# The order in which TensorE reads the keys in the row-maximum passes of an attention kernel

## The chip, the cores and the metric

The kernel runs on one core of a Trainium2 chip. The metric is the device time of one execution in microseconds (us), the median over the executions shown. The engines of the core are called PE (TensorE, matrix products), ACT (ScalarE), DVE (VectorE), POOL (GpSimd) and SP (SyncE, which here issues DMAs). PE takes a stationary operand through a weight load (PEld) and streams a moving operand against it, column by column, from the on-chip memory SBUF into a bank of PSUM; a bank holds 512 float32 columns on each of 128 partitions.

## The reference, cut to what matters

```python
def _B_ref(x, wqkv, wo):          # x: 1 x 2048 x 1024, H = 32 heads of Dh = 32
    qkv = (x @ wqkv).reshape(B, S, 3, H, Dh).transpose(2, 0, 3, 1, 4)
    q, k, v = qkv[0], qkv[1], qkv[2]
    scores = jnp.einsum("bhqd,bhkd->bhqk", q, k) * (Dh ** -0.5)
    p = softmax(scores, axis=-1)
    o = jnp.einsum("bhqk,bhkd->bhqd", p, v)
    return o.transpose(0, 2, 1, 3).reshape(B, S, D) @ wo

g = sigmoid((x * gate_w).sum(-1, keepdims=True))
return g * _A_ref(x, A_wqkv, A_wo) + (1 - g) * _B_ref(x, B_wqkv, B_wo)
```

`_A_ref` is a linear attention of the same size (feature map, keys times values, a division by the sum of keys). Everything is float32. The softmax of block B subtracts the largest score of each row, so the kernel needs the maximum over 2048 keys for each query and head. A maximum doesn't depend on the order in which the keys come.

## The kernel before

The program is written by a planner in Python: several streams of work (generators) each offer their next step, the planner keeps a modelled time for every engine (`T`), and it appends the step that is furthest behind its due time and whose operands are modelled to be there. What comes out is one fixed order of instructions for each engine. The modelled price of one 512-column product is `MM = 0.2275`. Nothing of this runs on the chip; there the engines follow their queues and wait on semaphores.

The first stage (lines below 850) makes queries, keys and values of block B. The main stage runs four streams side by side:

- `maxima()`, the passes of the row maxima. For each of the 32 heads it goes through 64 pairs of a block of 128 queries (`t`, 16 of them) and a block of 512 keys (`j`, 4 of them). A pass is one product on line 1263: the stationary operand is a 128 x 128 block of the stacked queries `q`, the moving operand is `k[:, j * C:(j + 1) * C]`, 512 neighbouring keys (C = 512), and the result fills one PSUM bank. On line 1268 DVE reduces the bank to one maximum per query. Queries and keys are stored as high and low parts, stacked on the 128 partitions, in the type float32r.
- `heads_()` with `attend()`: the products of keys with queries on line 1405, the exponential on ACT (line 1408), sums of the exponentials on POOL (line 1490) and DVE (line 1506), and the products with the values on line 1555. The latter are plain float32; each of the program's 2048 products runs as two passes, which makes 4096 instructions, and four of them with 32 columns of weights each share the array.
- `linear()`: the projections of block A and the rest of block B's values, on lines 153, 156 and 158, three products for each of eight row blocks, with transposes on line 1049 and the small key-value products on line 938.
- `output()`: the last projection.

The maxima of a head are made about one head and 12 passes (`LEAD`) ahead of its exponentials. After the 64 passes of a head, `rows(h)` turns the 16 columns of maxima with one small transpose on line 1280, and two short DMAs write them into the stacked operand, so that the products on line 1405 come out with the maximum subtracted. A pass takes a bank with `take`, and `give` sets it free when the reduction on DVE has read it; seven banks go around (six of a ring and one that is lent while it is idle). The lines around the change:

## Time and profile before

| | |
|---|---|
| time, median of 2 runs | 2806.33 us (2805.76 to 2806.9) |
| span of the profiled execution, first to last instruction | 2803.6 us |
| mean granted clock of TensorE | 1.000 |
| first and last start of a pass of the row maxima (line 1263) | 432.0 and 2572.4 us |
| passes of the row maxima | 2048, busy 739.0 + 62.8 us |
| reductions behind them (line 1268) | 2048, busy 1314.3 us, 684 ns each |

The page gives, for an engine, the time in which at least one of its instructions is under way, and its share of the span. In its list of groups a row names the source line, the engine, the operation, the tile written and the tiles read, the shapes and the count; after the first bar come the busy time of the whole group in us and the mean of one in ns, after the second the idle time of the engine just before these instructions and what ended it. Products overlap in the array, so the busy time of one is longer than the interval from one start to the next. No separate time of the profiled execution is given beside its span; what lies around the span is taken from the runs' median.

### The profile page before, as it was taken

The numbers are of one execution on the slowest core, as the hardware profiler recorded it, in microseconds if no ns is written. First come the engines' busy times: TensorE is split into PE (matmuls) and PEld (weight loads), VectorE is DVE, ScalarE is ACT, GpSimd is POOL, SyncE is SP. The second block draws the span as 40 slices with busy tenths as digits, with TensorE's granted clock in tenths as the row PEclk, the third lists the DMA queues.
The fourth block names the chain that finished last, engine by engine and source line by source line (L and its number), as shares of the span: only waits on it lengthen the run. The fifth ranks groups of instructions, "written<-read, shape, count | busy, mean of one in ns | idle before, by whom it ended". The sixth has DMA issues, their size and how long they took to land.

```text
span 2803.6 us, 46986 instructions
## 1 busy us (share of the span) xinstructions
PE 2794.3 (100%) x15880; PEld 2040.4 (73%) x15880; DVE 2327.5 (83%) x3745; ACT 1640.2 (59%) x3095; POOL 2104.4 (75%) x1150
## 2 busy tenths in 40 slices
PE   9999999999999999999999999999999999999999
PEld 8888888776677767777667777776676667666687
DVE  7978956888888888888888888888887888886688
ACT  5334323666676666666666676676666666666522
POOL 0642543799999999999899988889889988888000
PEclk9999999999999999999999999999999999999999
DMA  8997979433444334333433444455575555544774
GB/s 286 314 327 232 319 225 287 153 99 107 104 120 109 99 95 125 99 102 97 135 98 102 107 129 133 148 175 178 176 222 145 147 159 150 144 122 150 253 234 152
DMA packets 403340, 459.52 MB, mean 164 GB/s; under 512 B 106894, under 2 KB 234894, under 8 KB 401308
## 3 DMA queue, kind: packets, MB, share of 16 engines
q1 hardware_dynamic: 381084, 419.03, 48.6%
q0 software_dynamic: 22016, 37.50, 6.3%
q8 instruction: 126, 2.06, 0.3%
q14 instruction: 114, 0.93, 0.1%
HBM read 314.31 MB, written 127.66 MB: 158 GB/s over the span
## 4 chain that ended last, share of the span: by engine, by line
PE 91%; DMA 3%; DVE 1%; issue 1%; SPq 0%; ACT 0%; ACTq 0%; DVEq 0%
PE bank L1405 17%; PE bank L1263 17%; PE bank L1555 16%; PE bank L153 13%; PE bank L158 13%; PE bank L156 13%; PE bank L1327 1%; PE bank L1049 1%; DMA big<-wv 1%; SPq L170 0%; DMA big<-ra 0%; DMA xs<-big 0%; PE bank L938 0%; DMA mid<-in_xT 0%; DMA extra<-in_xT 0%
## 5 line engine op out<-in xcount | busy, mean ns | idle before, releaser
L1490 POOL TENSOR_TENSOR big<-big,big 128x512 f32<-128x512 f32 (+2 forms) x694 | 1642.0, 2370 | 106.9 <-ACT big L1408 63.8
L1268 DVE TENSOR_REDUCE mx<-bank 128x1 f32<-128x512 f32 x2048 | 1314.3, 684 | 301.1 <-PE bank L1263 297.5
L1408 ACT ACTIVATE big<-bank 128x512 f32<-128x512 f32 x2048 | 1180.0, 602 | 427.8 <-PE bank L1405 362.4
L1405 PE MATMUL bank<-big,big 128*128 128x512 f32 x1888 | 741.5, 394 | 0.1
L1263 PE MATMUL bank<-big,big 128*128 128x512 f32 x1888 | 739.0, 391 | 0.0
L153 PE MATMUL bank<-big,big 128*128 128x512 f32 x1576 | 616.0, 391 | 2.8 <-ACT big L302 1.2
L156 PE MATMUL bank<-big,big 128*128 128x512 f32 x1576 | 614.2, 390 | 0.0
L158 PE MATMUL bank<-big,big 128*128 128x512 f32 x1572 | 613.2, 390 | 0.2 <-DMA big<-xs 0.2
L1555 PE MATMUL bank<-big,mid 128*32 128x512 f32 x4096 | 454.2, 593 | 0.0
L1405 PEld LDWEIGHTS bank<-big,big 128*128 128x128 f32 x1888 | 354.0, 188 | 124.7 <-issue 47.4
L1263 PEld LDWEIGHTS bank<-big,big 128*128 128x128 f32 x1888 | 354.5, 188 | 73.7 <-ACT big L1408 1.4
L153 PEld LDWEIGHTS bank<-big,big 128*128 128x128 f32 x1576 | 296.0, 188 | 69.5 <-ACT big L302 2.6
L158 PEld LDWEIGHTS bank<-big,big 128*128 128x128 f32 x1572 | 295.1, 188 | 63.6 <-DVE big L297 1.0
L156 PEld LDWEIGHTS bank<-big,big 128*128 128x128 f32 x1576 | 295.9, 188 | 61.3 <-DVE big L297 0.2
L1555 PEld LDWEIGHTS bank<-big,mid 128*32 128x32 f32 x4096 | 143.6, 110 | 264.3 <-issue 264.0
L1506 DVE TENSOR_TENSOR bank<-bank,big 128x512 f32<-128x512 f32 x364 | 252.2, 693 | 5.5 <-ACT big L1408 3.3
L302 ACT CAST big<-mid 128x512 fp32r<-128x512 f32 (+1 forms) x157 | 92.9, 618 | 122.5 <-DVE mid L1674 66.0
L1486 POOL TENSOR_TENSOR big<-big,big 128x1536 f32<-128x1536 f32 (+1 forms) x31 | 123.4, 3980 | 40.3 <-ACT big L1408 40.1
L153 PE MATMUL bank<-big,xh 128*128 128x512 f32 x376 | 147.0, 391 | 0.6 <-DVE mx L1268 0.6
L158 PE MATMUL bank<-big,xh 128*128 128x512 f32 x376 | 146.9, 391 | 0.3 <-DMA xh<-xs 0.3
L156 PE MATMUL bank<-big,xh 128*128 128x512 f32 x376 | 146.8, 390 | 0.0
L1563 ACT COPY mid<-bank 128x512 f32<-128x512 f32 x32 | 18.8, 587 | 212.8 <-PE bank L1555 205.8
(165 smaller groups left out, 2226.4 us busy)
## 6 DMA issues: line engine op xcount, KB each, us to landing
big<-xs SPq DMA_DIRECT2D x288, 256.0 KB
big<-qk SPq DMA_DIRECT2D x690, 64.0 KB
xh<-xs SPq DMA_DIRECT2D x144, 256.0 KB
qk<-mid SPq DMA_DIRECT2D x128, 256.0 KB
big<-oA SPq DMA_DIRECT2D x84, 256.0 KB
xs<-big SPq DMA_DIRECT2D x64, 256.0 KB
oA<-mid SPq DMA_DIRECT2D x64, 256.0 KB
big<-big POOLq DMA_DIRECT2D x50, 256.0 KB, 5.4
```

Of the source, the lines that this page charges most:

```text
L153: yield nc.tensor.matmul(ps, sh, mh_, start=(kt == 0), stop=False)
L156: yield nc.tensor.matmul(ps, sh, ml_, start=False, stop=(late and last))
L158: yield nc.tensor.matmul(ps, sl, mh_, start=False, stop=last)
L302: nc.scalar.copy(hi, src)
L1263: nc.tensor.matmul(bank[b], q[:, t % TPC * P:(t % TPC + 1) * P], k[:, j * C:(j + 1) * C], start=True, stop=True)
L1268: nc.vector.tensor_reduce(m[:, t, j:j + 1], bank[b], AX.X, ALU.max)
L1405: nc.tensor.matmul(bank[b], k[:, t * P:(t + 1) * P], q_cols(h, j), start=True, stop=True)
L1408: nc.scalar.activation(pr_t[i][:, j * C:(j + 1) * C], bank[b], AF.Exp, scale=SCALE)
L1486: nc.gpsimd.tensor_add(lacc[:, :qp], pr(0)[:, :qp], pr(1)[:, :qp])
L1490: nc.gpsimd.tensor_add(lacc[:, sl], lacc[:, sl], pr(t)[:, sl])
L1506: nc.vector.tensor_add(lacc[:, qp:] if t == NT - 1 else l_b[:, :n], l_b[:, :n], src)
L1555: nc.tensor.matmul(av_b[j * DH:(j + 1) * DH, :], v[:, t, :], pr(t)[:, j * C:(j + 1) * C], start=(t == 0), stop=(t == NT - 1))
```

## The change

Each of the passes of line 1263 reads its 512 keys in an order that depends on the head's number modulo 8, which I call its kind:

| kind | order in which the 512 keys enter |
|---|---|
| 0 | as before, one after the other |
| 1, 2, 3, 4 | with a step of 2, 4, 16 or 32 keys: first keys 0, n, 2n and so on, then 1, n + 1 and so on |
| 5 | pairs of neighbours, each second pair first (keys 0, 1, 4, 5, ...), then the others |
| 6 | runs of 16 neighbours, each second run first, then the others |
| 7 | as before, but as two products of 256 keys into the two halves of the bank |

The result is written to the bank from column 0 to column 511 in every kind, so for kinds 1 to 6 the scores stand in the bank in another order. The reduction reads all 512 of them as before. There are 32 heads, so each kind has 4 heads of 64 passes. A key is 4 bytes. The planner's price of a pass is left at `MM`. This is the whole diff:

```diff
+    def key_order(kind, to, keys):
+
+        if kind == 7:
+            return [(to[:, :HC], keys[:, :HC]), (to[:, HC:], keys[:, HC:])]
+        if kind in (1, 2, 3, 4):
+            n = (2, 4, 16, 32)[kind - 1]
+            return [(to.rearrange("p (n c) -> p n c", n=n), keys.rearrange("p (c n) -> p n c", n=n))]
+        if kind in (5, 6):
+            e = (2, 16)[kind - 5]
+            return [(to.rearrange("p (n c e) -> p n c e", n=2, e=e), keys.rearrange("p (c n e) -> p n c e", n=2, e=e))]
+        return [(to, keys)]
+
     def maxima():
...
                 end = use("pe", MM, free[b])
-                nc.tensor.matmul(bank[b], q[:, t % TPC * P:(t % TPC + 1) * P], k[:, j * C:(j + 1) * C],
-                                 start=True, stop=True)
+                rows_ = q[:, t % TPC * P:(t % TPC + 1) * P]
+                keys = k[:, j * C:(j + 1) * C]
+                for to, mov in key_order(h % 8, bank[b], keys):
+                    nc.tensor.matmul(to, rows_, mov, start=True, stop=True)
                 s_done[0] += 1
                 fill(end + LATE)
```

Here HC is 256. In the changed file the passes are on line 1278 instead of 1263, the reduction is on 1282 instead of 1268, and line 1405 has become 1419.

On PE, where the passes of head 6 end and those of head 7 (kind 7) begin, the program before has these instructions; a name like bank_244 is a PSUM bank, the two names after the arrow are the stationary and the moving operand, and the last column is the size of the result:

```order
L1263 MATMUL bank_239<-big_207,big_206 128x512
L1405 MATMUL bank_241<-big_208,big_209 128x512
L1263 MATMUL bank_244<-big_209,big_208 128x512
L156 MATMUL bank_238<-big_222,big_210 128x512
L158 MATMUL bank_238<-big_222,big_210 128x512
L1405 MATMUL bank_243<-big_208,big_209 128x512
L1263 MATMUL bank_240<-big_209,big_208 128x512
```

The changed program has at the same place on PE:

```order
L1278 MATMUL bank_239<-big_207,big_206 128x512
L1419 MATMUL bank_241<-big_208,big_209 128x512
L1278 MATMUL bank_244<-big_209,big_208 128x256 x2
L156 MATMUL bank_238<-big_222,big_210 128x512
L158 MATMUL bank_238<-big_222,big_210 128x512
L1419 MATMUL bank_243<-big_208,big_209 128x512
L1278 MATMUL bank_240<-big_209,big_208 128x256 x2
```

Each pass of head 7 has become two instructions with the same operands, and nothing else has moved; the passes of head 6 (the first row) look as before, since the order of their keys isn't part of such a row.

On DVE, which reduces the banks that these passes fill, a piece of the program before reads as follows (mx is the tile of the maxima, big_4148 one of the exponentials):

```order
L1268 TENSOR_REDUCE mx_199<-bank_242 128x1
L1268 TENSOR_REDUCE mx_199<-bank_239 128x1
L1268 TENSOR_REDUCE mx_199<-bank_238 128x1
L1506 TENSOR_TENSOR bank_245<-bank_245,big_4148 128x512
L1268 TENSOR_REDUCE mx_199<-bank_243 128x1
```

The same piece in the changed program:

```order
L1282 TENSOR_REDUCE mx_199<-bank_242 128x1
L1282 TENSOR_REDUCE mx_199<-bank_239 128x1
L1282 TENSOR_REDUCE mx_199<-bank_238 128x1
L1520 TENSOR_TENSOR bank_245<-bank_245,big_4148 128x512
L1282 TENSOR_REDUCE mx_199<-bank_243 128x1
```

Only the line numbers differ: the same banks are reduced in the same order.

## The prediction

> **What bounds the kernel now.** I read the page from the top: the busy shares of the engines, the 40 slices, the chain that ended last, the costliest groups.

> ```profile
> span 2803.6 us, 46986 instructions
> PE 2794.3 (100%) x15880; PEld 2040.4 (73%) x15880; DVE 2327.5 (83%) x3745; ACT 1640.2 (59%) x3095; POOL 2104.4 (75%) x1150
> PE   9999999999999999999999999999999999999999
> PEclk9999999999999999999999999999999999999999
> PE 91%; DMA 3%; DVE 1%; issue 1%; SPq 0%; ACT 0%; ACTq 0%; DVEq 0%
> ```

> TensorE (PE) is busy in every slice, at the full granted clock, and carries 91% of the chain. Outside its busy time there are only 2803.6 - 2794.3 = 9.3 us of the whole span. So whatever lengthens a matmul has nowhere to hide, and whatever another engine gains or loses below PE's pace costs nothing. A "busy" PE could still be a PE that waits inside its pipeline, so I checked the pace in the timeline of PE alone, in a stretch of twenty full-size matmuls in a row (first and last row shown):

> ```profile
> 1007.55 0.39 PE L1405 MATMUL bank<-big,big 128*128 128x512 f32 x1
> ...
> 1011.86 0.39 PE L156 MATMUL bank<-big,big 128*128 128x512 f32 x1
> ```

> The starts lie (1011.86 - 1007.55) / 19 = 0.2268 us apart. Each is busy for 0.39 us, because the next enters while the last still drains; the price of one more matmul is thus its interval, not its busy time. The passes of the row maxima are line 1263, and the reduction that waits for each is line 1268. These groups, from the page and from the list of groups with shapes kept apart, carry the rest of the argument:

> ```profile
> L1268 DVE TENSOR_REDUCE mx<-bank 128x1 f32<-128x512 f32 x2048 | 1314.3, 684 | 301.1 <-PE bank L1263 297.5
> L1263 PE MATMUL bank<-big,big 128*128 128x512 f32 x1888 | 739.0, 391 | 0.0
> L1263 PE MATMUL bank<-big,extra 128*128 128x512 f32 x160 | 62.8, 393 | 0.0
> L1555 PE MATMUL bank<-big,mid 128*32 128x512 f32 x4096 | 454.2, 593 | 0.0
> L938 PE MATMUL bank<-mid,mid 128*32 128x32 f32 x1024 | 15.7, 199 | 0.0
> L1263 PEld LDWEIGHTS bank<-big,big 128*128 128x128 f32 x1888 | 354.5, 188 | 73.7 <-ACT big L1408 1.4
> ```

> Passes of line 1263 number 1888 + 160 = 2048: 32 heads by 64. Their moving operand is 512 neighbouring keys of 4 bytes. VectorE (DVE) waits 297.5 us in all for these matmuls; PE never waits for VectorE there (0.0). The next view gives the busy time by stretch; this row is a steady one:

> ```profile
> 600.00:1000.00 400.00, 399.97 (x2585) 280.92 (x2576) 347.06 (x587) 263.62 (x509) 371.85 (x184) 1.00 0.38 103
> ```

> After the length come PE, PE's weight loads, VectorE, ScalarE and GpSimd: PE is full, VectorE at 347.06 of 400, GpSimd at 371.85 of 400. GpSimd is the next engine behind PE, 7% short of it.

> **The change part by part.** The kind is the head's number modulo 8, so each kind has 4 heads and 4 x 64 = 256 passes. Kind 0 is unchanged. The planner still charges a pass MM = 0.2275, so the order of work on all engines stays as it was; only kind 7 puts a second matmul behind the first. Nothing moves past a queue, no DMA is added, and no wait is added: the reduction still waits for one release, that of the last matmul into its bank. The maximum doesn't depend on the order of the keys, and the bank is still written from column 0 to 511.

> *Kind 7, two matmuls of 256 keys.* It adds 256 matmuls and 256 weight loads. A 32-column product (line 938) takes 199 ns and a 512-column one 391, so a column costs (391 - 199) / 480 = 0.40 ns. Of the interval of 227 ns the columns are 205, and 22 are a fixed part that each half pays anew: 2 x (102 + 22) = 248, which is 21 ns more. 256 x 0.021 = 5.5 us. The lower bound is 0, if the fixed part overlaps. The upper bound is one weight load (188 ns, the last row above) in the open for each pair: 256 x 0.188 = 48 us, plus the 5.5. What decides between them is the shortest run of full-width loads in the trace, the four transposes of 128 columns, each with a load of its own:

> ```profile
> 1708.28 0.60 PE L1049 MATMUL bank<-ident,mid 128*128 128x128 f32 x4
> 1708.63 0.48 PE L1263 MATMUL bank<-big,big 128*128 128x512 f32 x1
> ```

> Four loads and matmuls are in before 0.35 us have passed, and the matmul behind them runs 0.48 instead of 0.39, so about 0.44 us for four. A load every 0.11 us keeps up with halves of 0.124 us. I take 5.5 us.

> *Kinds 1 to 6, one matmul with stepped keys.* Instructions, columns and weight loads stay as they are. What can change is the pace at which the moving operand comes out of SBUF. The trace of before has no matmul that reads with a step, so the price is bounded from both sides. Lower bound: 0, since the array still takes 512 columns, and nothing in fewer. A gain is excluded: nothing about a step makes 512 columns fewer. Upper bound from the nearest row: line 1555, the one whose columns enter at a slower pace. Four such passes of 512 columns share the array, and 4 x 454.2 / 4096 = 0.4436 us go by per group, against 0.2268 for line 1263: 0.217 us more. By its busy time it is 593 - 391 = 202 ns more. So a stream of 512 keys at half pace costs 0.20 to 0.22 us more; I call it 0.21.

> I take a mechanism in which a read of the memory brings several neighbouring keys at a time and a stream that uses only one of them drops to half pace. It is an assumption that this trace can't show. For it speaks that line 1263 must be given 512 x 4 bytes in 0.2268 us, 9.0 bytes a nanosecond in each partition, where one stream of line 1555 is given 512 x 4 in 0.4436, 4.6. No single stream of the trace is seen to get more than the first figure, and that one is of neighbouring keys. With steps of 4, 16 and 32 (kinds 2, 3, 4) no two keys in turn come from the same four, so I charge these the 0.21; with a step of 2, in pairs, and in runs of 16 (kinds 1, 5, 6) at least two in turn lie in one group of four, so I charge these nothing. The charge is 3 x 256 x 0.21 = 161.3 us, with 0 and 0.217 x 768 = 167 as ends for these three kinds. What would hide it would be slack of PE, and of that there are the 9.3 us above.

> [...]

> *Sum.* 2803.6 (the span of the execution shown) + 5.5 + 161.3 = 2970.4. The median of the runs shown, 2806.33, is 2.7 above that span, for what lies around it; I add it: **2973 us**, 5.9% more. In the slow heads GpSimd and VectorE get more slack, not less. The steps are in neighbouring heads, and this row of the source line that runs once a head gives their length:

> ```profile
> L1280 PE MATMUL bank<-ident,mneg x32: 270/271/275, 492.0 to 2574.4; 128*16 128x128 f32 x32
> ```

> (2574.4 - 492.0) / 31 = 67.2 us a head; a head of kinds 2 to 4 would take 64 x 0.21 = 13.4 us more, about 80.6.

> **The rivals.**

> *Steps are free* (ends on the other side: not slower). The operand's path reads ahead and gathers any 512 keys at the full pace. Then only kind 7 pays: 2803.6 + 5.5 + 2.7 = 2812. For it: PE never waits for an operand anywhere in this page, and the four streams of line 1555 together get 4 x 4.6 = 18.5 bytes a nanosecond from SBUF, so the memory has twice the supply of one stream. Against it: those are four streams with a path each, not one. The point from which it decides: the 2% mark is 56 us, less 5.5 for kind 7, over 768 passes, so a wide step that costs under 66 ns.

> *Only the widest steps pay*, 16 and 32: 2812 + 512 x 0.21 = 2919. It needs a reach of more than four keys; the page speaks neither for nor against it.

> *All stepped kinds pay half pace*, 1 to 5, because the pace of line 1263 is already the most that whole groups of neighbours give: 2812 + 1280 x 0.21 = 3081. The fixed 22 ns beside 205 ns of columns say that contiguous reads leave little to spare.

> *The same limit, in full*: if a group of four neighbours takes the time of four columns whatever of it is used, a step of 2 and pairs cost double and steps of 4 and more four times the columns: 2812 + 512 x 0.21 + 768 x 3 x 0.205 = 3392. Against it: no row shows a stream slower than half pace.

> *Kind 7 with its loads in the open* and free steps: 2812 + 48 = 2860, held off by the four transposes. That the change does nothing is no rival: a stepped read can't be folded into a plain one while the bank is written in order.

> **How the numbers follow.** Forecast 0.32; free 0.31; only the widest 0.11; all at half pace 0.09; four times 0.14; open loads 0.02; faster 0.01, for which nothing speaks. A measurement of this kernel can tell about 2% (56 us) from no change. Slower by more: 0.32 + 0.11 + 0.09 + 0.14 = 0.66; within: 0.31 + 0.02 = 0.33; faster: 0.01. The likeliest's own range is 2955 (0.19 a pass) to 3025 (0.217, and kind 7 at its upper bound). The range on record reaches to the free case and to all kinds at half pace, 2806 to 3085, and holds 0.32 + 0.31 + 0.11 + 0.09 + 0.02 = 0.85 of the cases; what is left out is the fourfold case and the faster one.

> **What would show it right or wrong.** In the changed profile the passes of the maxima should fall into groups: kinds 0, 1, 5, 6 with starts 0.227 us from the matmul before, kinds 2, 3, 4 about 0.44, halves of kind 7 about 0.124. Their time on the chain should grow by 161 us, all heads of kinds 2 to 4 should take 80 us and the others 67, and VectorE's wait for the passes should grow by about as much. Steps that are free show in heads of equal length; a wider effect shows in heads 1, 5, 9, 13 and so on. The forecast is wrong if kind 1 or 5 pays, if the price rises with the step from 4 to 32, or if kind 7 costs more than 0.05 us a pass.

## The result and the profile after

The changed kernel takes 3110.06 us (median of 2 runs, 3108.28 to 3111.84) against 2806.33 before: ratio 1.108, 95% interval 1.105 to 1.111. It is slower, as forecast, but by 304 us instead of 167, and 25 us above the top of the range.

These are the page's lines of the changed kernel that answer to those of before: span, busy shares, slices, chain, and the groups of the passes (now line 1278), of the reduction (1282) and of the scores (1419).

```profile
span 3110.1 us, 47538 instructions
PE 3101.1 (100%) x16136; PEld 2080.0 (67%) x16136; DVE 2387.4 (77%) x3745; ACT 1664.8 (54%) x3095; POOL 2105.2 (68%) x1150
PEclk9999999999999999999999999999999999999999
PE 98%; DMA 1%; DVE 0%; issue 0%; ACT 0%; SPq 0%; DVEq 0%; ACTq 0%
L1282 DVE TENSOR_REDUCE mx<-bank 128x1 f32<-128x512 f32 x2048 | 1372.5, 686 | 524.2 <-PE bank L1278 512.0
L1278 PE MATMUL bank<-big,big 128*128 128x512 f32 (+1 forms) x2128 | 998.6, 488 | 0.5 <-ACT big L1422 0.5
L1419 PE MATMUL bank<-big,big 128*128 128x512 f32 x1888 | 767.8, 408 | 0.0
```

The scores' row before was, on its page:

```profile
L1405 PE MATMUL bank<-big,big 128*128 128x512 f32 x1888 | 741.5, 394 | 0.1
```

PE is still the bound: 3110.1 - 3101.1 = 9.0 us lie outside its busy time, 9.3 before. The granted clock is 1.00, as before, so the clock explains nothing. The passes have grown, and VectorE now waits 512.0 us for them instead of 297.5. VectorE, ScalarE and GpSimd do the same work in a longer span. The mean of the passes hides what happened, because it mixes eight kinds. The busy time by stretch, for the passes of line 1278 alone and cut at the heads 8 to 15, shows one kind in each row (length of the stretch, then PE busy with its count, weight loads with theirs, clock, DMA share, GB/s; a row can hold one instruction of its neighbour):

```profile
1017.20:1081.40 64.20, 25.02 (x64) 12.03 (x65) 1.00 0.39 101
1081.40:1160.30 78.90, 39.48 (x65) 12.16 (x65) 1.00 0.36 97
1160.30:1240.40 80.10, 39.95 (x64) 12.11 (x65) 1.00 0.35 94
1240.40:1317.40 77.00, 37.91 (x64) 12.23 (x65) 1.00 0.30 80
1317.40:1395.50 78.10, 38.03 (x64) 12.11 (x65) 1.00 0.32 83
1395.50:1474.30 78.80, 39.53 (x64) 12.08 (x65) 1.00 0.30 77
1474.30:1539.30 65.00, 25.93 (x64) 12.04 (x65) 1.00 0.48 131
1539.30:1604.30 65.00, 25.53 (x128) 24.09 (x129) 1.00 0.38 98
```

Five heads are long, not three: kinds 1 (step of 2) and 5 (pairs) last as long as the steps of 4, 16 and 32. The weight loads of kinds 0 to 6 don't change (12 us a head; kind 7 has twice as many), so they aren't what has grown. Whether it is the read of the keys or the write of the scores is tested below. The instructions of line 1278 in four of these stretches (minimum, median and maximum of the busy time in ns) show how long one pass is busy, for kinds 0, 2, 4 and 5:

```profile
L1278 PE MATMUL bank<-big,big x48: 388/389/398, 1026.5 to 1081.0; 128*128 128x512 f32 x48
L1278 PE MATMUL bank<-big,big x64: 619/622/810, 1160.4 to 1238.9; 128*128 128x512 f32 x64
L1278 PE MATMUL bank<-big,big x64: 592/594/596, 1317.5 to 1394.0; 128*128 128x512 f32 x64
L1278 PE MATMUL bank<-big,big x64: 610/615/692, 1395.6 to 1473.1; 128*128 128x512 f32 x64
```

Against 389 ns, a step of 4 is busy 233 ns longer, a step of 32 205, pairs 226. From here on, "full pace" is about 390 ns and "half pace" about 600.

These are busy times; the price, as in the prediction, is the interval from one start to the next. A pass of kind 2, the product behind it and the one behind that, from PE's timeline:

```profile
1169.53 0.62 PE L1278 MATMUL bank<-big,big 128*128 128x512 f32 x1
1169.97 0.41 PE L1419 MATMUL bank<-extra,big 128*128 128x512 f32 x1
1170.22 0.39 PE L153 MATMUL bank<-big,big 128*128 128x512 f32 x1
```

The pass takes 0.44 us of PE instead of 0.227, and the product behind it, though read plainly, 0.25. Over the whole profile, with the time from each start on PE to the next put down to the instruction that starts it, the passes take 264 us more than before, the scores 29 and the projections 14, which is the whole of the longer span. The median pass costs 209, 213, 189, 189 and 210 ns more in kinds 1 to 5, and a product behind it 22 to 28 ns.

### The profile page after: what moved, and what is told of

It is laid out like the page before. It is cut to its first block, busy times and chain, and to the rows that moved or that the text cites. A ratio compares the mean times of both kernels' runs of the same rounds, so it can differ in the third digit from the quotient of the medians.

```text
span 3110.1 us, 47538 instructions
## 1 busy us (share of the span) xinstructions
PE 3101.1 (100%) x16136; PEld 2080.0 (67%) x16136; DVE 2387.4 (77%) x3745; ACT 1664.8 (54%) x3095; POOL 2105.2 (68%) x1150
## 2 busy tenths in 40 slices
PE   9999999999999999999999999999999999999999
## 4 chain that ended last, share of the span: by engine, by line
PE 98%; DMA 1%; DVE 0%; issue 0%; ACT 0%; SPq 0%; DVEq 0%; ACTq 0%
PE bank L1278 24%; PE bank L1419 16%; PE bank L1569 14%; PE bank L153 14%; PE bank L156 14%; PE bank L158 14%; PE bank L1341 0%; PE bank L1049 0%; DMA big<-ra 0%; PE bank L938 0%; DMA big<-xs 0%; PE bank L1333 0%; PE bank L1009 0%; PE bank L1294 0%; DMA big<-in_b_wqkv 0%
## 5 line engine op out<-in xcount | busy, mean ns | idle before, releaser
L1282 DVE TENSOR_REDUCE mx<-bank 128x1 f32<-128x512 f32 x2048 | 1372.5, 686 | 524.2 <-PE bank L1278 512.0
L1422 ACT ACTIVATE big<-bank 128x512 f32<-128x512 f32 x2048 | 1199.4, 601 | 695.5 <-PE bank L1419 659.8
L1278 PE MATMUL bank<-big,big 128*128 128x512 f32 (+1 forms) x2128 | 998.6, 488 | 0.5 <-ACT big L1422 0.5
L1419 PE MATMUL bank<-big,big 128*128 128x512 f32 x1888 | 767.8, 408 | 0.0
L153 PE MATMUL bank<-big,big 128*128 128x512 f32 x1576 | 619.3, 393 | 3.2 <-ACT big L302 1.7
L156 PE MATMUL bank<-big,big 128*128 128x512 f32 x1576 | 617.8, 392 | 0.0
L158 PE MATMUL bank<-big,big 128*128 128x512 f32 x1572 | 616.5, 392 | 0.2 <-DVE big L297 0.2
L1278 PEld LDWEIGHTS bank<-big,big 128*128 128x128 f32 x2128 | 400.8, 189 | 105.7 <-issue 14.6
L1419 PEld LDWEIGHTS bank<-big,big 128*128 128x128 f32 x1888 | 356.4, 189 | 143.5 <-issue 66.7
L153 PEld LDWEIGHTS bank<-big,big 128*128 128x128 f32 x1576 | 301.0, 191 | 116.1 <-issue 53.7
L156 PEld LDWEIGHTS bank<-big,big 128*128 128x128 f32 x1576 | 300.7, 191 | 106.4 <-issue 53.4
L158 PEld LDWEIGHTS bank<-big,big 128*128 128x128 f32 x1572 | 299.4, 190 | 106.6 <-issue 50.5
L156 PE MATMUL bank<-big,xh 128*128 128x512 f32 x376 | 148.3, 394 | 0.0
L297 DVE TENSOR_TENSOR big<-mid,big 128x512 fp32r<-128x512 f32 (+1 forms) x126 | 87.6, 714 | 65.6 <-ACT big L302 56.5
```

What stands on the lines that cost most here:

```text
L153: yield nc.tensor.matmul(ps, sh, mh_, start=(kt == 0), stop=False)
L156: yield nc.tensor.matmul(ps, sh, ml_, start=False, stop=(late and last))
L158: yield nc.tensor.matmul(ps, sl, mh_, start=False, stop=last)
L1278: nc.tensor.matmul(to, rows_, mov, start=True, stop=True)
L1282: nc.vector.tensor_reduce(m[:, t, j:j + 1], bank[b], AX.X, ALU.max)
L1419: nc.tensor.matmul(bank[b], k[:, t * P:(t + 1) * P], q_cols(h, j), start=True, stop=True)
```

## The experiments

Each kernel gives an order of the keys to each kind of head, so that one profile holds eight measurements. Its diff is to the changed kernel, except for "Other steps" and the last three, which start from the kernel before. Lines that a diff takes out of `key_order` aren't shown, and "..." stands for lines left out. The parts of the change and the last three kernels were timed several times; the others ran once, and what is read from them is the busy time of a pass in their profiles, all at a granted clock of 1.00. The theories (G, J, W, later T) are named in the expectation in which each first appears.

**The change in three parts.** In the first kernel only kinds 1 and 5 have their changed order, in the second only kinds 2 to 4, in the third only kinds 6 and 7; all other heads read as before:

```diff
-                for to, mov in key_order(h % 8, bank[b], keys):
+                for to, mov in key_order(h % 8 if h % 8 in (1, 5) else 0, bank[b], keys):
```

(in the second kernel `(2, 3, 4)`, in the third `(6, 7)`).

> Only kinds 1 (step of 2 keys) and 5 (pairs) read in another order; all other heads read as before. The forecast's mechanism (two keys in turn from one group of four cost nothing): 2806 us. Theory G (a read brings four neighbouring keys, and a pass that doesn't use all four in turn falls to two array cycles a column, whatever the step): 512 passes by 0.226 us of longer busy time and about 0.009 us on the matmul behind each, 2806 + 120 = 2926 us.

> Only kinds 2, 3 and 4 (steps of 4, 16, 32 keys). The forecast's term for them: 768 passes by 0.21 us, 2806 + 161 = 2967 us. Theory G with the longer busy times of the changed profile (233, 203 and 205 ns) and 0.009 us on the matmul behind each: 2806 + 171 = 2977 us.

> Only kinds 6 (runs of 16) and 7 (two products of 256 keys). The forecast's terms: 0 and 5.5 us, 2812 us. From the changed profile: 256 by 0.018 + 0.003 us and 256 by 0.007 + 0.006 us, 2806 + 9 = 2815 us. If the three parts add up, the three kernels' differences to before sum to the whole 304 us; if the parts hinder each other through another engine, they sum to less.

Measured beside 2807.5 us for the kernel before: kinds 1 and 5 2928.88 us (ratio 1.043, 1.041 to 1.0445), kinds 2 to 4 2979.32 (1.061, 1.0595 to 1.063), kinds 6 and 7 2816.64 (1.003, 1.002 to 1.0045). The differences are 121.4, 171.8 and 9.1 us and add up to 302 of the 304 us. So nothing is hidden and nothing is lost between the parts. Theory G's numbers (2926, 2977, 2815) hold to 3 us. They were worked out from the busy times of the changed profile, so their agreement shows that the parts add up, and not yet that G is right. The forecast's 0 for kinds 1 and 5 is refuted.

**Runs of other lengths.**

```diff
...
+        n, e = ((1, 512), (2, 4), (2, 8), (2, 32), (2, 64), (2, 128), (8, 4), (8, 16))[kind]
+        return [(to.rearrange("p (n c e) -> p n c e", n=n, e=e), keys.rearrange("p (c n e) -> p n c e", n=n, e=e))]
```

> Kind 0 reads plainly; kinds 1 to 5 read alternate runs of 4, 8, 32, 64 and 128 keys, kinds 6 and 7 runs of 4 and 16 of which each eighth is next. Theory G: any run of four or more in whole groups is at full pace, median busy time 389 to 410 ns in all kinds, time under 2830 us. Theory J (each break in the row of addresses costs the 18 ns / 32 = 0.56 ns that runs of 16 show, at most up to double pace): runs of 4 take 389 + 72 = 461 ns, of 8 425, of 16 407, of 32 398, of 64 394, of 128 391; time 2806 + 55 = 2861 us. If the group is larger than four keys, runs of 4 take 615 ns as pairs do, and the time is 2925 us or more.

The kernel took 2824.93 us. The passes with alternate runs of 4 keys, and with runs of 4 of which each eighth is next:

```profile
L1271 PE MATMUL bank<-big,big x65: 389/393/397, 1007.8 to 1071.4; 128*128 128x512 f32 x65
L1271 PE MATMUL bank<-big,big x48: 398/411/415, 1339.4 to 1394.8; 128*128 128x512 f32 x48
```

Runs of 4 read at full pace (393), where pairs took 615. The other kinds, with runs of 8 to 128 keys, take 389 to 397 ns. Theory J, which prices each jump, wanted 461 for runs of 4 and falls. The small rest (runs of 4 a wide way apart: 411; runs of 16 in the change: 407) isn't explained.

**Where a run begins.** Here 4 to 32 of the 512 keys of a pass are left out of the maximum.

```diff
+    WIDTH = (508, 508, 508, 508, 504, 504, 480, 480)
...
+        at, e = ((0, 0), (1, 0), (2, 0), (3, 0), (0, 4), (2, 4), (0, 16), (2, 16))[kind]
+        to, keys = to[:, :WIDTH[kind]], keys[:, at:at + WIDTH[kind]]
+        if not e:
+            return [(to, keys)]
+        return [(to.rearrange("p (n c e) -> p n c e", n=2, e=e), keys.rearrange("p (c n e) -> p n c e", n=2, e=e))]
...
-                nc.vector.tensor_reduce(m[:, t, j:j + 1], bank[b], AX.X, ALU.max)
+                nc.vector.tensor_reduce(m[:, t, j:j + 1], bank[b][:, :WIDTH[h % 8]], AX.X, ALU.max)
```

> Every pass leaves 4 to 32 of its 512 keys out of the maximum. Kinds 0 to 3 read 508 neighbouring keys from key 0, 1, 2 or 3 on; kinds 4 and 5 read 504 keys in alternate runs of 4 from key 0 or 2 on; kinds 6 and 7 read 480 keys in alternate runs of 16 from key 0 or 2 on. Theory G: kinds 0 to 3 are alike within a few ns (387 to 395), kind 4 is near 400, kind 5 cuts each group in two and takes about 610 ns as pairs do, kind 7 takes some 20 ns more than kind 6. Theory J (only breaks count): the start makes no difference anywhere, kinds 4 and 5 are equal, kinds 6 and 7 are equal.

Four rows: neighbouring keys from key 2 on, runs of 4 from key 0 on, runs of 4 from key 2 on, runs of 16 from key 2 on.

```profile
L1276 PE MATMUL bank<-big,big x64: 386/395/575, 1092.3 to 1156.5; 128*128 128x508 f32 x64
L1276 PE MATMUL bank<-big,big x64: 388/391/393, 1221.8 to 1285.7; 128*128 128x504 f32 x64
L1276 PE MATMUL bank<-big,big x64: 602/616/686, 1287.1 to 1364.6; 128*128 128x504 f32 x64
L1276 PE MATMUL bank<-big,big x64: 427/437/616, 1430.2 to 1496.1; 128*128 128x480 f32 x64
```

The same runs of 4 take 391 ns when they begin at a multiple of four keys and 616 when each lies across two such groups. A plain read hardly cares where it begins (390 to 395). Runs of 16 from key 2 on take 437 ns and from key 0 on 391, which is 46 more where some 20 had been expected. So what counts in this read are fixed groups of four keys, 16 bytes, as theory G says: 391 ns inside them, 616 across them.

**The write side.**

```diff
...
+        n, e = ((1, 512), (2, 2), (8, 2), (32, 2), (2, 4), (2, 16), (2, 2), (2, 16))[kind]
+        to = to.rearrange("p (c n e) -> p n c e", n=n, e=e)
+        if kind in (6, 7):
+            return [(to, keys.rearrange("p (c n e) -> p n c e", n=n, e=e))]
+        return [(to, keys.rearrange("p (n c e) -> p n c e", n=n, e=e))]
```

> Kinds 1 to 5 read the keys plainly and write the scores to PSUM out of order: in pairs at a step of 4, 16 and 64 columns, in runs of 4 and of 16; kinds 6 and 7 read and write in pairs and in runs of 16, so that the scores stand where they stood before. Theories G and J (only the read costs): kinds 1 to 5 take 389 ns, kind 6 615 and kind 7 407; time 2806 + 60 + 5 = 2871 us. Theory W (the cost comes from the form of the pattern or from the write): kinds 1 to 3 take 600 ns or more as well, time 2806 + 4 x 60 = 3046 us or more.

The kernel took 2874.33 us, 2871 expected from the reads alone. Pairs written at a step of 64 columns from a plain read take 389 ns; pairs read and written take the 615 of the reads:

```profile
L1274 PE MATMUL bank<-big,big x48: 388/389/397, 1159.5 to 1213.0; 128*128 128x512 f32 x48
L1274 PE MATMUL bank<-big,big x48: 612/615/633, 1353.9 to 1419.8; 128*128 128x512 f32 x48
```

The other kinds that read plainly take 389 ns as well. Written in pairs or longer runs, the scores cost nothing, and nor does the pattern's form: the price lies in the read. Theory W falls.

**Plain float32.** Kinds 1 to 6 take both operands as plain float32, in two passes; their orders are named in the expectation.

```diff
...
+                as_ = f32 if 1 <= h % 8 <= 6 else (lambda a: a)
+                for to, mov in key_order(h % 8, bank[b], as_(keys)):
+                    nc.tensor.matmul(to, as_(rows_), mov, start=True, stop=True)
```

> Kinds 1 to 6 take the same operands as plain float32, in two passes of two array cycles a column: kind 1 plainly, 2 to 4 with steps of 2, 4 and 32, 5 in pairs, 6 in runs of 16. Theory G as a limit on keys (a key out of its group takes two array cycles to come): plain float32 takes these two cycles anyway, so kinds 2 to 6 are as long as kind 1, each pass near 590 ns, and the time is 2806 + 6 x 256 x (2 x 0.44 - 0.227) = 3809 us. If the step doubles whatever pace there is, kinds 2 to 5 take twice kind 1: 3809 + 4 x 256 x 0.88 = 4710 us.

The kernel took 4271.73 us, between the two expectations. First the two instructions of one product of kind 1 from PE's timeline, then single instructions of kinds 1 (neighbours), 2 (step of 2), 3 (step of 4) and 5 (pairs):

```profile
1379.75 1.02 PE L1277 MATMUL bank<-big,big 128*128 128x512 f32 x2
L1277 PE MATMUL bank<-big,big x129: 389/591/595, 1368.4 to 1472.4; 128*128 128x512 f32 x129
L1277 PE MATMUL bank<-big,big x128: 609/612/616, 1473.5 to 1580.1; 128*128 128x512 f32 x128
L1277 PE MATMUL bank<-big,big x96: 1058/1070/1079, 1609.2 to 1744.5; 128*128 128x512 f32 x96
L1277 PE MATMUL bank<-big,big x128: 609/612/617, 1906.6 to 2012.5; 128*128 128x512 f32 x128
```

The two instructions are busy 1.02 us together and one alone 0.59, so the second starts 0.43 us behind the first: a column of plain float32 takes 0.84 ns, against 0.2268 / 512 us = 0.44 ns in the float32r passes. That is what the expectations mean by two array cycles and one. Here a step of 2 and pairs cost 21 ns, and a step of 4 costs 479 (a step of 32, not shown, 446; runs of 16 nothing). So in plain float32, at half the speed, two keys from each group suffice: what the forecast had assumed for the float32r passes, which with the same orders need 226 ns more. Theory G has no place for that difference.

**Other steps.**

```diff
...
+        n = (1, 3, 5, 8, 64, 256, 2, 1)[kind]
+        if n == 1:
+            return [(to, keys)]
+        to, keys = to.rearrange("p (n c) -> p n c", n=n), keys.rearrange("p (c n) -> p n c", n=n)
+        return [(to[:, i], keys[:, i]) for i in range(2)] if kind == 6 else [(to, keys)]
...
+                if h % 8 == 7:
+                    rows_ = q.rearrange("p (c n) -> p n c", n=TPC)[:, t % TPC, :]
```

> Kinds 1 to 5 read with steps of 3, 5, 8, 64 and 256 keys (3 and 5 leave two keys out of the maximum), kind 6 reads two products of 256 keys, each with a step of 2, and kind 7 has plain keys but a stationary operand whose queries have a step of 4, so that the maxima belong to other queries. Theory G: kinds 1 to 5 all 590 to 625 ns, without growth along the step; kind 6 two halves of about 0.117 + 0.113 = 0.23 us interval each; kind 7 as plain, 389 ns, since the weight load has some 0.1 us to spare beside the matmul before. Time 2806 + 256 x (5 x 0.225 + 0.236) = 3154 us. If wider steps meet busy parts of the memory, 64 and 256 are longer than 8 by more than 20 ns; if a stepped stationary read also halves its pace, the loads of kind 7 go from 188 to 290 ns or more.

The kernel took 3128.21 us, 3154 expected. Steps of 3, 64 and 256, and the plain keys with a stepped stationary operand (its weight load and its product):

```profile
L1279 PE MATMUL bank<-big,big x65: 389/611/615, 1082.8 to 1160.8; 128*128 128x510 f32 x64, 128*128 128x512 f32 x1
L1279 PE MATMUL bank<-big,big x64: 696/714/727, 1317.7 to 1401.3; 128*128 128x512 f32 x64
L1279 PE MATMUL bank<-big,big x64: 377/378/462, 1403.0 to 1464.8; 128*128 128x512 f32 x64
L1279 PEld LDWEIGHTS bank<-big,big x64: 307/309/312, 1545.4 to 1609.2; 128*128 128x128 f32 x64
L1279 PE MATMUL bank<-big,big x64: 387/394/596, 1545.6 to 1609.4; 128*128 128x512 f32 x64
```

Theory G is wrong in one place that matters: the step of 256 (0, 256, 1, 257, ...) never has two neighbours in turn, and it is *faster* than the plain read, 378 ns against 389. Steps of 5 and 8 (612 and 593 ns) and the two products of 256 keys with a step of 2 (402 ns each, where plain halves take 278) came out as expected; the step of 64 is slower than the 590 to 625 ns of theory G. The stepped weight load takes 309 ns instead of 188, and the product that needs it 394 instead of 389, so the load is all but hidden behind the product before it.

```diff
...
+        if kind in (1, 4):
+            n = 256 if kind == 1 else 128
+            return [(to.rearrange("p (n c) -> p n c", n=n), keys.rearrange("p (c n) -> p n c", n=n))]
+        if kind in (2, 3, 6):
+            e = {2: 4, 3: 2, 6: 16}[kind]
+            return [(to.rearrange("p (c e n) -> p c e n", n=2, e=e), keys.rearrange("p (c n e) -> p c e n", n=2, e=e))]
+        if kind == 5:
+            return [(to.rearrange("p (c m e) -> p c m e", m=2, e=2), keys.rearrange("p (m c e) -> p c m e", m=2, e=2))]
+        if kind == 7:
+            return [(to.rearrange("p (n c m) -> p n c m", n=2, m=2), keys.rearrange("p (m c n) -> p n c m", n=2, m=2))]
```

> Kind 0 plain. The keys enter in these orders, with the scores written in the order of entry: kind 1: 0, 256, 1, 257 and so on; kind 2: in each eight 0, 4, 1, 5, 2, 6, 3, 7; kind 3: in each four 0, 2, 1, 3; kind 4: a step of 128, so 0, 128, 256, 384, 1 and so on; kind 5: pairs from two halves, 0, 1, 256, 257, 2, 3; kind 6: in each 32 keys 0, 16, 1, 17 and so on; kind 7: 0, 256, 2, 258, 4, 260 and so on, then the odd keys. Theory T (two readers take the columns in turn, one the even ones of the order of entry and one the odd ones, each at one key in two array cycles, and each needs two keys in turn from one group of four neighbours): kinds 1, 2, 3, 6 and 7 at full pace, 378 to 392 ns, kinds 4 and 5 at half pace, 590 ns or more. Theory G (all four neighbours of a group in turn): kinds 1, 2, 4, 5, 6 and 7 at half pace, 590 ns or more, kind 3 full. A theory by which only the width of the step counts has kind 4 as fast as kind 1, which was 378 ns.

Kinds 2, 4, 5 and 7:

```profile
L1280 PE MATMUL bank<-big,big x64: 377/379/567, 1075.4 to 1138.2; 128*128 128x512 f32 x64
L1280 PE MATMUL bank<-big,big x64: 432/436/445, 1202.8 to 1269.4; 128*128 128x512 f32 x64
L1280 PE MATMUL bank<-big,big x64: 488/496/569, 1270.8 to 1340.8; 128*128 128x512 f32 x64
L1280 PE MATMUL bank<-big,big x64: 388/390/581, 1405.0 to 1468.0; 128*128 128x512 f32 x64
```

All five kinds that theory T has at full pace came out so (1, 3 and 6, not shown, at 379, 390 and 378 ns). Kind 7 is the sharpest: a step of 2, which costs 226 ns when read alone, is free when two such streams alternate. Theory G, which wanted 590, is done. So is a rule that only counts how many groups four columns in a row touch: it is two for a step of 2 and for pairs (615) as for 0, 256, 2, 258 (390). But for kinds 4 and 5, in which a reader leaves a group and comes back to it, theory T was wrong: they came out between full and half pace (436 and 496), not at half. One more run asked whether a reader keeps a group that it left, or whether the distance of the places matters:

```diff
...
+        m, d = ((4, 4), (4, 8), (4, 16), (4, 32), (4, 64), (8, 4), (8, 32))[kind - 1]
+        return [(to.rearrange("p (x c m) -> p x c m", m=m, c=d), keys.rearrange("p (x m c) -> p x c m", m=m, c=d))]
```

> The keys of blocks enter in turn from m places that lie d keys apart: kinds 1 to 5 with m = 4 and d = 4, 8, 16, 32, 64 (for d = 4: 0, 4, 8, 12, 1, 5, 9, 13, 2 and so on), kinds 6 and 7 with m = 8 and d = 4 and 32. In the order of entry the even columns then alternate between two groups of four (m = 4) or go around four (m = 8), and so do the odd ones. Theory T in its strict form (two keys in turn from one group, for the even and for the odd columns each): half pace, 590 ns or more, for all seven. T with a memory (each reader keeps a group for a while, which explains the 437 ns of m = 4, d = 128): kinds 1 to 5 at 437 ns or less and alike, kinds 6 and 7 slower. T with places that hinder each other by their distance: kinds 1 to 5 grow with d from about 390 to 437 ns, and m = 8 with d = 32 is slower than with d = 4, as the 714 ns of m = 8, d = 64 is slower than the 594 ns of a step of 32.

Four places 4 and 64 keys apart, then eight places 4 and 32 keys apart:

```profile
L1273 PE MATMUL bank<-big,big x64: 429/430/433, 1048.0 to 1113.7; 128*128 128x512 f32 x64
L1273 PE MATMUL bank<-big,big x64: 432/436/516, 1316.4 to 1382.0; 128*128 128x512 f32 x64
L1273 PE MATMUL bank<-big,big x48: 637/639/643, 1395.3 to 1462.5; 128*128 128x512 f32 x48
L1273 PE MATMUL bank<-big,big x64: 596/599/785, 1463.7 to 1539.9; 128*128 128x512 f32 x64
```

With two groups in turn to a reader the pass costs 40 to 47 ns whatever the distance (the three kinds not shown take 429 to 432 ns); with four groups it is at half pace or slower. The strict form of theory T is refuted by the first. That a reader keeps something of a group over a short detour fits, but isn't shown; the distance isn't the cause of the 45 ns. Two things stay open: kind 5 of the run before, also with two groups to a reader, costs 107 ns, and eight places take 639, 599 and 714 ns when they lie 4, 32 and 64 keys apart (the last is the step of 64), which doesn't go by distance.

**Using it.** If 0, 256, 1, 257 is faster than the plain order, the kernel before can be made faster. The first kernel reads all 2048 passes so. The second does it for the scores as well, and ScalarE puts the columns back as it reads the bank. The third adds the stream of projections, whose weights are stored so that this order brings them in their natural one (two more places that split weights are changed like the one shown).

```diff
+    def two(a):
+        return a.rearrange("p (c n) -> p n c", n=HC)
+    def flat(a):
+        return a.rearrange("p (n c) -> p n c", n=HC)
+    def put(a):
+        return a.rearrange("p (n c) -> p n c", n=2)
+    def taken(a):
+        return a.rearrange("p (c n) -> p n c", n=2)
...
-                nc.tensor.matmul(bank[b], q[:, t % TPC * P:(t % TPC + 1) * P], k[:, j * C:(j + 1) * C],
+                nc.tensor.matmul(flat(bank[b]), q[:, t % TPC * P:(t % TPC + 1) * P], two(k[:, j * C:(j + 1) * C]),
...
-                nc.tensor.matmul(bank[b], k[:, t * P:(t + 1) * P], q_cols(h, j), start=True, stop=True)
+                nc.tensor.matmul(flat(bank[b]), k[:, t * P:(t + 1) * P], two(q_cols(h, j)), start=True, stop=True)
...
-                nc.scalar.activation(pr_t[i][:, j * C:(j + 1) * C], bank[b], AF.Exp, scale=SCALE)
+                nc.scalar.activation(put(pr_t[i][:, j * C:(j + 1) * C]), taken(bank[b]), AF.Exp, scale=SCALE)
...
-        nc.scalar.copy(hi, raw)
+        hi, lo, raw_ = put(hi), put(lo), taken(raw)
+        nc.scalar.copy(hi, raw_)
...
-                for m, _ in enumerate(three(ps, stat, (wpart(k, 0), wpart(k, 1)), k)):
+                for m, _ in enumerate(three(flat(ps), stat, (two(wpart(k, 0)), two(wpart(k, 1))), k)):
```

> The kernel before, with all 2048 passes of the maxima in the order 0, 256, 1, 257 and so on. Theory T: each pass takes 216 ns instead of 227, as the head with a step of 256 did; 2048 x 0.011 = 22.5 us less, 2785 us, ratio 0.992. If what a pass saves is lost again (DVE or the banks become the limit), 2806 us.

> The same order for the 2048 products of the scores too, with ScalarE reading the bank with a step of two columns so that the exponentials stand in their old places. Theory T: another 22.5 us less, 2762 us, ratio 0.984, if ScalarE's reads with a step of 2 cost less than its idle time. If ScalarE's stepped read of PSUM doubles its 602 ns, ScalarE becomes the bound and the time rises above 2806 us.

> In addition the 3456 products of the stream of projections take their weights, stored so that the order 0, 256, 1, 257 and so on brings the columns in their natural order; the weights' two split operations read with a step of 2. Theory T: 3456 x 0.011 = 38 us less again, 2724 us, ratio 0.970, if the splits on ScalarE, VectorE and GpSimd don't become longer.

Measured beside 2807.58 us: 2796.72 us (ratio 0.996, 0.995 to 0.997), 2778.65 (0.989, 0.988 to 0.991) and 2756.61 (0.982, 0.980 to 0.983). All three beat the kernel before, the last by 51 us or 1.8%, but the steps gain 10.9, 18.1 and 22.0 us where 22.5, 22.5 and 38 were expected. ScalarE's reads with a step of 2 cost nothing (busy 1634.6 us in the second kernel, 1640.2 before). In the first kernel the passes did gain: 380 ns busy (line 1275) against 391. But the products around them, still read plainly, lost some of it: the scores (line 1417) take 397 ns against 394. Added up from start to start on PE, the passes gain 25 us, as expected, the scores lose 7 and the projections 10; in the second kernel passes and scores gain 23 and 24, and the projections lose 17.

```profile
L1417 PE MATMUL bank<-big,big 128*128 128x512 f32 x1888 | 748.1, 397 | 0.5 <-DMA big<-ml 0.5
L1275 PE MATMUL bank<-big,big 128*128 128x512 f32 x1888 | 717.7, 380 | 0.3 <-ACT big L1420 0.2
```

In the third kernel, where neighbours in the queue all read in the new order, seventeen in a row start (1011.80 - 1008.35) / 16 = 0.2156 us apart, against 0.2268 before (first and last of them, from PE's timeline):

```profile
1008.35 0.38 PE L1418 MATMUL bank<-big,big 128*128 128x512 f32 x1
...
1011.80 0.38 PE L1276 MATMUL bank<-big,big 128*128 128x512 f32 x1
```

Its page has PE busy for 2737.1 of a span of 2752.8 us, so the time outside grew from 9.3 to 15.7 us. Of the 32 us that lack to the expected 83, about 23 lie in intervals of more than 0.28 us between starts of full-size products: beyond 0.227 us each, these add up to 53 us there and to 30 before. What those products wait for wasn't followed further.

## Why the prediction was wrong

**The step that failed** is the one by which kinds 1 and 5 were free: "with a step of 2, in pairs, and in runs of 16 (kinds 1, 5, 6) at least two in turn lie in one group of four, so I charge these nothing". Kinds 1 and 5 cost 121.4 us. The count of keys per group was taken along the order of entry; the runs fit a count over every second column of that order better (a step of 2 takes 615 ns alone and 390 where two such streams alternate). In the picture of theory T, two keys in turn go to different readers, and a step of 2 leaves each reader one key of a group, just like a step of 4. Runs of 16 were rightly taken as nearly free, at 18 ns a pass. The prediction had named this very sign of being wrong, that kind 1 or 5 pays.

**The group of four was right, the count in it was not.** That four neighbouring keys make a group, and that two keys in turn from one suffice, was the author's assumption; no row of the profile before shows either. The group shows where a run begins (391 ns against 616). That two suffice shows in plain float32: 612 ns with two keys of a group, 1070 with one, against 591. For the float32r passes, two hits next to each other in the order of entry weren't enough (615 against 389). That is what theory T adds.

**The wide steps** were charged 161.3 us and cost 171.8. Half pace was right for them, and no price rose from a step of 4 to one of 32 (213, 189 and 189 ns from start to start, 0.197 us a pass where 0.21 was charged). What the sum lacked is the loss on the product behind a slow pass, 22 to 28 ns. A price slightly too high and a missing term cancel in part, so that 161.3 came so close is partly luck.

**Kind 7** was charged 5.5 us, and kinds 6 and 7 together cost 9.1; its halves start 0.116 to 0.119 us apart, so their weight loads are hidden, as the four transposes had said.

**What hides it**: nothing, as forecast. The time outside PE's busy time stayed at 9 us, and the parts add up to the whole.

**The rivals.** The one that happened was "all stepped kinds pay half pace", with 3081 us and a chance of 0.09. It lacked the runs of 16 and above all the losses on the products around the slow passes: 29 us in all. What spoke for it was there to be read: the fixed 22 ns beside 205 ns of columns said that a plain read leaves little to spare, and yet the forecast gave it less than a tenth. The fourfold case is refuted for float32r by kind 2 (622 ns), and steps are not free. The range ended at the rival's bare sum, without the losses on the products behind, and so it missed by 25 us. Two smaller points: by its own terms the likeliest's range is 2958 to 3027 and not 2955 to 3025, and "a gain is excluded" doesn't hold of every step, as the step of 256 showed (378 ns against 389).

Theory T is inferred from paces: it says which of some 40 orders are at full pace, and the runs can't show the readers themselves. The 45 and 107 ns of a detour and the 639 and 714 ns of eight places aren't in it.

## What to carry to other kernels

A moving operand of float32r that is read in single keys or pairs from one place ran at half pace here, 0.2 us more per 512 columns, whether the step was 2 or 32; if an order must be changed, change it in runs of four or more from a multiple of four (389 to 411 ns here, against 389), or on the write side, which cost nothing here in pairs (389). Two streams that alternate column by column, each through neighbours, were read faster here than one (0.2156 against 0.2268 us). Where the order of the columns is free, as in a maximum, this needs no other change, but among plain products about half of the gain was lost again (10.9 of 22.5 us stayed). Price a slow product with the loss on the one behind it (22 to 28 ns here). Before charging a new access pattern, find out in which unit the hardware counts: one profile with a pattern per head answers that in a single run.

## What was not expected of the hardware

- The plain read of 512 neighbours isn't the fastest: 389 ns busy, against 378 for 0, 256, 1, 257. From start to start a product takes 0.2268 us before, where all of them read plainly, and 0.2156 in the last kernel, where neighbours in the queue all read in the new order.
- A plain product right behind one with another read order takes longer: from start to start 249 to 255 ns behind a pass at half pace, where 227 is usual between plain ones. Among passes in the order 0, 256, 1, 257 the plain scores are busy for 397 ns instead of 394.
- A stationary operand with a step of 4 takes 309 ns to load instead of 188, and almost none of it is seen while a product of 512 columns runs before it (394 ns against 389).
- Scores written to PSUM in pairs 64 columns apart cost nothing (389 ns).
